# A hot expert's later tokens looked up straight from their ranks, with a new list of prologue steps

## The chip, the core and the metric

The program runs on one core of a Trainium2 chip. The metric is the time of one execution in microseconds (us) of device time, and lower is better. The kernel before has a median of 582.75 us over three runs (581.17 to 585.8).

The engines are TensorE (PE in the rows, and PEld for its weight loads), VectorE (DVE), ScalarE (ACT), GpSimd (POOL) and SyncE (SP). Each works through its own queue in order and waits for the others by semaphores. SyncE here mostly issues DMA transfers.

## The reference: an attention layer and two layers of experts

```python
kv = einsum('bhsd,bhse->bhde', k, v)            # 4 batches, 8 heads, 576 positions, 64 wide
out = einsum('bhsd,bhde->bhse', q, kv)
x = out / sqrt(mean(out * out, -1) + 1e-06) * g_norm   # then 2304 tokens of 512
# layer 1 (moe) and, on its result, layer 2 (moe2, with 576 places for each expert)
logits = x @ w_gate;  expert = argmax(logits);  gate = softmax(logits)[expert]   # 8 experts
out[tokens of e] = gate * (relu(x[tokens of e] @ w1[e]) @ w2[e])   # 512 -> 1024 -> 512
```

## The kernel before: attention as a listed prologue, then experts in blocks

Tokens lie in 18 units of 128 (UNITS, line 30): for each pair of batches eight units from the bodies and one from both tails. Units form four groups, 0-3, 4-8, 9-12 and 13-17 (GROUPS, line 28). A group shares one reciprocal root, one pass for the logits and one store of its rows to the tensor x1d in memory.

The prologue has no scheduler. ORDER (line 69) is a list of tokens; the loop at line 567 calls one small function for each, and the call appends its instructions to the queues of the engines. So the list sets the order on all engines at once. Names used below: Lk, Lv, Lq and Lt load k, v, q and the tails; kvB.P is one quarter of the product of k and v of batch B (10 matmuls, line 368); kvout, kvt, kvtc, kvg and kvgc prepare that product for use, with the gate's weights folded in (kvgc, line 392, is the last); oU is unit U's output (line 400), evU its evacuation (line 279 or 277), sqU the squares and ssqU their sums (lines 431 to 437); ra, rs, rb make the scale of a group (lines 449 to 463), lp and lg its logits (lines 478 and 485), st stores it. wN issues 2N matmuls whose result nobody reads. W loads a piece of expert weights, sh and sl split it into a high and a low part (lines 1105 and 1108).

Matmuls on expert weights are done as three products of such parts. Experts' tokens are done in blocks. Block 0 is 128 early tokens of the "hot" expert, the one most often chosen in the first nine units. `lead` (line 772, steps a) finds these tokens once groups 0 and 1 have logits: ranks come from a triangular matmul, and a one-hot lookup matmul (line 856) turns ranks into row numbers. Its weights' loads wait on SyncE's queue for the expert's number (ordia, line 839). The prologue also computes block 0: p (first product), t (turn), z (second product), y, lt, ll.

`final` (line 942, steps f) does all other tokens, once group 3 has logits (line 596 on): choice of expert, ranks for eight experts, each expert's rank and base, the one-hot tiles lo (line 647) and hv (line 658), the lookup matmuls (line 666), row numbers gi (line 677). Then block 1, the hot expert's next 224 tokens, is gathered from x1d (line 1137), normalised (nrm, line 1179), turned (xt, lines 1187 to 1199), and the loop of `moe` (line 1421) starts its matmuls at line 1211. That loop runs blocks 1, 2, ... of layer 1 and then layer 2, and steps generators such as `final` between the matmuls. Block 2 is the next expert's, of 320 tokens.

Of the kernel before, what the change touches and what calls it, by code (L numbers as in the profile page):

```python
# [70 lines left out]
Lk1.1 Lv1.1 Lv2.0 wgb kv1.0 kv1.2 ct2 Lq0.0 kvg0 eye Lk2.1 Lt2.0 iotawA kv1.3 kvout1A Lk2.0 foursD csD Lq1.0 triP
kvgc0 o2 ev2D Lq2.1 o1 Lq1.1 ev1A sq1A Lq2.0 o3 kvt1 kvtc1D ev3A o0 ssq1 kvg1 sq3A ssq3 ev0A sq0A kvgc1 o5 ev5A ssq0
sq2P o4 Lt0.1 ev4A ssq2 o6 ra0 rs0 rb0 ev6A sq6A ssq6 o7 sq5P Lt1.1 ev7A sq4A Lv2.1 ssq5 Lq3.1 kv2.1 kv2.0 o8 kv2.3
kv2.2 Lv3.1 lp0D sq7P ssq7 ev8A sq8A ssq4 ssq8 lg0 Lv3.0 st0 ra1 rs1 rb1 lp1D kvout2A w4.42386 kvt2 w1.42420 kvtc2A
w2.42371 kvg2 kvgc2 lg1 a1 o10 ev10A o9 st1 w1.42338 a2 w1.42406 ev9A a3 o11 o12 ev11A sq11P a4 a5 a6 ssq11 sq9A a7
Lk3.1 Lk3.0 kv3.1 kv3.0 kv3.3 kv3.2 sq10A ssq10 ssq9 Lq3.0 a8 ev12A sq12A W0 a9 firstD W1 ssq12 nrm0.0P Lt2.1 ra2 a10
w2.42387 kvout3D kvt3 kvtc3D rs2 rb2 w6.4256 lp2P kvg3 kvgc3 o13 W2 W3 f1 sh0 a11 sh1 ev13A o14 lg2 sl0 W4 sl1 W5
sq13P sh2 ev14A o16 ssq13 xt0.0 sl2 sh3 ev16D sq14P a12 ssq14 o17 ev17A sq16A ssq16 sl3 sq17A ssq17 sh4 w2.42422 o15
ev15A sq15A p0.0 sh5 a13 p0.1 st2 sl4 ssq15 ra3 rs3 p0.2 a14 rb3 sl5 W6 lp3P p0.3 lg3 f2 W7 t0.0 w4.42431 w3.42356 sh6
# [96 lines left out]
class Kernel:  # L176
# [109 lines left out]
    def attention(self):  # L286
# [3 lines left out]
        with ExitStack() as s:  # L290
# [157 lines left out]
            def ra(g):  # L448
                V.tensor_scalar(
                    out=small(0, g), in0=ssq[g].rearrange("p c h -> p (c h)"), scalar1=64e-6, scalar2=None, op0=ALU.add  # L450
                )

            def rs(g):
                A.activation(out=small(1, g), in_=small(0, g), func=ACTF.Sqrt)

            def rb(g):
                vv, r0, t = (small(i, g) for i in range(3))
# [1479 lines left out]
```

## Time and profile before

| what | us |
|---|---|
| median of three runs | 582.75 |
| the profiled execution | 584.3 |
| span in its profile, first to last instruction | 582.5 |
| TensorE busy in that span | 552.8 |
| first matmul on block 1 | 99.31 |

The profiled execution is 1.55 us above the median. The span splits at 99.31 us: ahead of it stands the prologue, whose order is written in the list; after it stands the loop over blocks.

### The profile page before, as it was taken

To read this page: it belongs to the slowest core of one execution; us is meant where nothing else is said; L and a number is where in the kernel's file an instruction comes from. 1 tells how busy PE (TensorE), PEld (TensorE's weight loads), DVE (VectorE), ACT (ScalarE), POOL (GpSimd) and SP (SyncE) were. 2 spreads that over 40 slices of the span, in tenths; PEclk is the share of its full clock that TensorE was granted. 3 is DMA by queue.
4 is the path that set the end of the run, shared out by engine and by line. 5 is a ranking of instruction groups with operands and counts; after the bars stand their busy time and mean duration, and the time that the engine had idled before them with its cause. 6 is when DMAs were issued, how large, how long until landed. Compare 5 with 4: busy or idle time off the path is not lost.

```text
span 582.5 us, 10758 instructions
## 1 busy us (share of the span) xinstructions
PE 552.8 (95%) x4130; PEld 525.1 (90%) x4130; DVE 330.2 (57%) x741; ACT 243.8 (42%) x421; POOL 182.4 (31%) x187
## 2 busy tenths in 40 slices
PE   8898898999999999999998999999999999999995
PEld 6887776998999999999987998989899999989994
DVE  0466983467867576767688586275147662211370
ACT  0456622436455555564645342244243532111440
POOL 1032225066625243433000101203322726543341
PEclk8999899999999999999999898999999999999998
DMA  9996746055556465656555434236234655768631
GB/s 305 399 381 217 264 144 193 3 178 168 179 172 205 157 203 172 213 176 200 175 181 166 134 111 167 72 93 234 88 101 153 202 188 177 257 238 265 242 127 39
DMA packets 34231, 106.89 MB, mean 184 GB/s; under 512 B 6665, under 2 KB 6795, under 8 KB 34172
## 3 DMA queue, kind: packets, MB, share of 16 engines
q1 hardware_dynamic: 24432, 81.90, 41.8%
q0 software_dynamic: 7072, 19.48, 10.7%
q10 hardware_dynamic: 2667, 4.75, 2.4%
q8 instruction: 34, 0.56, 0.4%
q14 instruction: 26, 0.20, 0.1%
HBM read 91.77 MB, written 14.60 MB: 183 GB/s over the span
## 4 chain that ended last, share of the span: by engine, by line
PE 69%; DVE 15%; issue 6%; ACT 5%; DMA 2%; POOL 1%; POOLq 0%; SPq 0%; ACTq 0%; DVEq 0%; another core or an unknown queue 0%
PE hps L1211 8%; PE hps L1212 8%; PE hps L1213 8%; PE acc L1211 7%; PE acc L1212 7%; PE acc L1213 7%; PE acc L1209 5%; PE hps L1209 4%; PE yps L1341 3%; DVE w1l L1108 3%; DVE w2l L1108 2%; PE xps L1187 2%; PE kv L368 2%; PE o L400 2%; PE sp L666 1%
## 5 line engine op out<-in xcount | busy, mean ns | idle before, releaser
L1211 PE MATMUL hps<-xh,w1h 128*128 128x256 f32 (+9 forms) x480 | 141.5, 295 | 1.0 <-ACT xh L1195 0.6
L1212 PE MATMUL hps<-xl,w1h 128*128 128x256 f32 (+9 forms) x480 | 139.0, 290 | 0.6 <-DVE xl L1199 0.5
L1213 PE MATMUL hps<-xh,w1l 128*128 128x256 f32 (+9 forms) x480 | 138.6, 289 | 0.0
L1232 ACT ACTIVATE hh<-hps 128x256 fp32r<-128x256 f32 (+12 forms) x144 | 54.4, 380 | 150.1 <-PE hps L1213 97.6
L1211 PE MATMUL acc<-hh,w2h 128*128 128x224 f32 (+8 forms) x352 | 104.6, 297 | 0.1
L1212 PE MATMUL acc<-hl,w2h 128*128 128x224 f32 (+8 forms) x352 | 103.0, 293 | 0.8 <-issue 0.8
L1213 PE MATMUL acc<-hh,w2l 128*128 128x224 f32 (+8 forms) x352 | 103.1, 293 | 0.0
L1211 PEld LDWEIGHTS hps<-xh,w1h 128*128 128x128 f32 x480 | 91.0, 190 | 3.0 <-issue 1.5
L1212 PEld LDWEIGHTS hps<-xl,w1h 128*128 128x128 f32 x480 | 91.1, 190 | 1.7 <-DVE xl L1199 1.3
L1213 PEld LDWEIGHTS hps<-xh,w1l 128*128 128x128 f32 x480 | 91.1, 190 | 0.0
L1234 DVE SCALAR_TENSOR_TENSOR hl<-hps,hh 128x256 fp32r<-128x256 f32 (+9 forms) x120 | 51.7, 436 | 63.7 <-ACT hh L1232 54.7
L1148 POOL DMA_INDIRECT xg<-x1d,gi x54 | 54.9, 1016 | 77.5 <-DVE xw L1162 63.5
L1108 DVE TENSOR_TENSOR w2l<-raw,w2h 128x1024 fp32r<-128x1024 f32 x52 | 66.2, 1276 | 19.2 <-ACT w2h L1105 18.1
L1396 POOL DMA_INDIRECT out_dram<-y,gi x44 | 50.5, 1149 | 70.9 <-DVE y L1392 56.8
L1108 DVE TENSOR_TENSOR w1l<-raw,w1h 128x1024 fp32r<-128x1024 f32 x52 | 64.0, 1248 | 13.6 <-ACT hh L1232 7.8
L1213 PEld LDWEIGHTS acc<-hh,w2l 128*128 128x128 f32 x352 | 67.2, 191 | 0.9 <-issue 0.9
L1211 PEld LDWEIGHTS acc<-hh,w2h 128*128 128x128 f32 x352 | 67.3, 191 | 0.3
L1212 PEld LDWEIGHTS acc<-hl,w2h 128*128 128x128 f32 x352 | 67.3, 191 | 0.2 <-issue 0.2
L1105 ACT ACTIVATE w2h<-raw 128x1024 fp32r<-128x1024 f32 x52 | 54.6, 1053 | 5.6 <-ACT y L1345 4.8
L1105 ACT ACTIVATE w1h<-raw 128x1024 fp32r<-128x1024 f32 x52 | 53.4, 1049 | 0.6 <-DMA raw<-in_moe_w_dram 0.5
L1137 POOL DMA_INDIRECT xg<-x2d,gi x21 | 20.0, 952 | 48.3 <-DVE gi L677 33.9
L1195 ACT ACTIVATE xh<-xps 128x512 fp32r<-128x512 f32 (+7 forms) x23 | 11.7, 512 | 45.3 <-PE xps L1187 31.2
(315 smaller groups left out, 818.9 us busy)
## 6 DMA issues: line engine op xcount, KB each, us to landing
raw<-in_moe_w_dram SPq DMA_DIRECT2D x104, 512.0 KB
w<-in_moe_w_dram SPq DMA_DIRECT2D x24, 512.0 KB
x1d<-xs POOLq DMA_DIRECT2D x4, 1056.0 KB
...
xg<-x1d,gi POOLq DMA_INDIRECT x59
```

What stands on the lines that cost most here:

```text
L1105: self.nc.scalar.activation(out=h, in_=t, func=ACTF.Copy)
L1108: self.nc.vector.tensor_tensor(out=l, in0=t, in1=h, op=ALU.subtract)
L1137: self.nc.gpsimd.indirect_dma_start(out=xg[:n], out_offset=None, in_=(self.X1, self.X2)[m][0:rows], in_offset=bass.IndirectOffsetOnAxis(ap ...
L1148: self.nc.gpsimd.indirect_dma_start(out=xg[:, g], out_offset=None, in_=(self.X1, self.X2)[m].rearrange("n (q x) -> (n q) x", q=4), in_offs ...
L1209: nc.tensor.matmul(out=out, lhsT=a[0], rhs=b[0], start=start, stop=stop)
L1211: nc.tensor.matmul(out=out, lhsT=a[0], rhs=b[0], start=start, stop=False)
L1212: nc.tensor.matmul(out=out, lhsT=a[0], rhs=b[1], start=False, stop=False)
L1213: nc.tensor.matmul(out=out, lhsT=a[1], rhs=b[0], start=False, stop=stop)
L1232: nc.scalar.activation(out=hh[:, fc, :], in_=ps, func=ACTF.Relu)
L1234: nc.vector.scalar_tensor_tensor(out=hl[:, fc, :], in0=ps, scalar=0.0, in1=hh[:, fc, :], op0=ALU.max, op1=ALU.subtract)
L1341: nc.tensor.matmul(out=ps[:n, j, :], lhsT=yt[:, dc, 128 * t:128 * t + n], rhs=self.iwg[:, dc, :], start=True, stop=True)
L1396: self.nc.gpsimd.indirect_dma_start(out=out, out_offset=bass.IndirectOffsetOnAxis(ap=rt["si4"][:, g - g0, t0 + t:t0 + t + 1].bitcast(U32), ...
```

## The change: what is looked up, when, and in which order

Four edits go together. First, `hot_block` finds the later tokens of the hot expert by itself: it needs only that expert's ranks, in two column groups (units 0-12, then 13-17), and its own lookup gives row numbers giq for block 1. The ranking of all experts follows after it in `final`, and its lookup and gi now come inside block 1; block 2 is then gathered from there. Second, the step ra is gone: the epsilon is a bias tile in the square root and an operand in rb. Third, the low part of a split may run on GpSimd, though every sl in the new list says D. Fourth, ORDER is another list; two of its lines stand in the diff. In it the constants iotaw (128x2944), first and eye are made on GpSimd, before on ScalarE, VectorE and GpSimd. The arrays' widths and the loop after block 2's first matmul are the same: each engine's queue holds the same instructions from there on.

```diff
--- before.py
+++ after.py
@@ -67,18 +67,19 @@ ORDER
-Lk0.1 Lv0.0 Lt1.0 Lv0.1 Lt0.0 Lk1.0 kv0.2 kv0.3 Lk0.0 w3.42407 kv0.1 kv0.0 kvout0D ct kvt0 kvtc0D Lv1.0 kv1.1 wg Lq0.1
...
+Lv0.1 Lk0.1 Lt0.0 Lt1.0 Lk0.0 Lv0.0 kv0.2 Lk1.0 kv0.3 Lv1.0 kv0.1 kv0.0 kvout0D ct kv1.1 kv1.0 Lk1.1 wg wgb Lv1.1
...
@@ -134,6 +135,9 @@
+HOT = (GROUPS[2][1], NCOL)
...
@@ -309,6 +314,7 @@
+            nc.gpsimd.memset(self.eps, 64e-6)
...
@@ -445,19 +451,18 @@
-            def ra(g):
-                V.tensor_scalar(
-                    out=small(0, g), in0=ssq[g].rearrange("p c h -> p (c h)"), scalar1=64e-6, scalar2=None, op0=ALU.add
+            def rs(g):
+                A.activation(
+                    out=small(1, g), in_=ssq[g].rearrange("p c h -> p (c h)"), func=ACTF.Sqrt, bias=self.eps
                 )
-            def rs(g):
-                A.activation(out=small(1, g), in_=small(0, g), func=ACTF.Sqrt)
...
-                V.tensor_tensor(out=t, in0=t, in1=vv, op=ALU.mult)
+                V.scalar_tensor_tensor(
+                    out=t, in0=ssq[g].rearrange("p c h -> p (c h)"), scalar=64e-6, in1=t, op0=ALU.add, op1=ALU.mult
+                )
...
@@ -510,8 +515,8 @@
-            def sl(_):
-                feed.low()
+            def sl(_, eng):
+                feed.low(eng)
...
@@ -939,6 +944,70 @@
+    def hot_block(self, hot, d, oh):
+        nc, V, t = self.nc, self.nc.vector, self.t
+        b = self.blocks[0][1]
+        nt = tiles_of(b.w)
+        val = self.tok1
+        own = t([128, NCOL], F16, "owna")
+        lo = self.mp.tile([128, 128, NCOL], F16, tag="yt", name="loq")
+        hv = self.rp.tile([128, 2, nt, NCOL], F16, tag="hvq", name="hvq")
+        for c0, c1 in zip((0,) + HOT, HOT):
+            n = c1 - c0
+            s = slice(c0, c1)
+            A3 = [128, n, E]
+            yield from self.chosen(0, c0, c1, d[:, s], oh[:, s])
+            w = t(A3, F32, "w")
+            V.tensor_tensor(out=w, in0=oh[:, s], in1=bc(hot, 1, A3), op=ALU.mult)
+            with nc.allow_low_precision("zeros and ones"):
+                V.tensor_reduce(out=own[:, s], in_=w, axis=AX.X, op=ALU.add)
+            yield
+            before = self.psum()[:, 0:c1 + n]
+            nc.tensor.matmul(out=before[:, c1:], lhsT=self.triw, rhs=own[:, s], start=True, stop=True)
+            nc.tensor.matmul(out=before[:, 0:c1], lhsT=self.onew, rhs=own[:, 0:c1], start=True, stop=True)
+            self.hold = True
+            yield
+            run = t([128, c1], F32, "runa")
+            V.tensor_tensor_scan(
+                out=run, data0=self.c(f"carry{c1}")[:, 0:c1], data1=before[:, 0:c1], initial=0.0,
+                op0=ALU.mult, op1=ALU.add,
+            )
+            rank = t([128, n], F32, "rank")
+            V.tensor_tensor(out=rank, in0=before[:, c1:], in1=run[:, s], op=ALU.add)
+            self.hold = False
+            yield
+            for i in range(nt):
+                V.scalar_tensor_tensor(
+                    out=hv[:, 0, i, s], in0=rank, scalar=128.0, in1=own[:, s], op0=(ALU.is_lt, ALU.is_ge)[i], op1=ALU.mult
+                )
+            low = t([128, n], F16, "low")
+            V.scalar_tensor_tensor(
+                out=low, in0=hv[:, 0, 1, s], scalar=-128.0, in1=rank, op0=ALU.mult, op1=ALU.add
+            )
+            yield
+            V.tensor_tensor(
+                out=lo[:, :, s], in0=self.iotaw[:, :, s], in1=bc(low, 1, [128, 128, n]), op=ALU.is_equal
+            )
+            yield
+            V.tensor_tensor(out=hv[:, 1, :, s], in0=hv[:, 0, :, s], in1=bc(val[:, s], 1, [128, nt, n]), op=ALU.mult)
+            yield
+        ps = self.psum()[:, 0:nt]
+        for j in range(NCOL):
+            nc.tensor.matmul(
+                out=ps, lhsT=lo[:, :, j], rhs=hv[:, 1, :, j], start=(j == 0), stop=(j == NCOL - 1)
+            )
+        self.hold = True
+        yield
+        gi = t([128, nt], I32, "giq")
+        V.tensor_scalar(out=gi, in0=ps, scalar1=float(OFF[0]), scalar2=None, op0=ALU.add)
+        self.hold = False
+        for i in range(nt):
+            n = min(128, b.w - 128 * i)
+            b.xgs.append((self.gather(0, gi, i, n), n))
+        yield
...
@@ -957,7 +1026,10 @@ final
-        yield from self.chosen(m, 0, ncol, d, oh)
+        if m == 0:
+            yield from self.hot_block(hot, d, oh)
+        else:
+            yield from self.chosen(m, 0, ncol, d, oh)
...
@@ -1019,7 +1091,9 @@
-        yield from self.index(m, rt, lo, hv, ncol, nt, "", self.blocks[m][-len(lay.blocks)].gather)
+        yield from self.index(
+            m, rt, lo, hv, ncol, nt, "", self.blocks[m][(2, -len(lay.blocks))[m]].gather
+        )
...
@@ -1444,7 +1518,7 @@ moe
-            if k and nb:
+            if k and nb and (m or "gi" in rt):
                 nb.gather()
...
@@ -1523,6 +1597,8 @@ moe
             if k == 1:
                 fin.run()
+                if not nb.xt:
+                    xs.extend(nb.x_steps())
...
```

What the new list does to the queues shows in three places. On TensorE, around the lookup of block 0 (ohe and triw are the ranks' operands, ot and lo the lookup's; kv_548 and kv_432 are the product of batch 3). Before, from the ranks of `lead` on:

```order
L794 MATMUL sp<-ohe,triw 128x72
L795 LDWEIGHTS onew
L795 MATMUL sp<-ohe,onew 128x72
L400 MATMUL o_117<-kvs,qkv 128x144 x4
L400 MATMUL o_116<-kvs,qkv 128x144 x4
L856 LDWEIGHTS lo_466
L856 MATMUL sp<-ot,lo_466 128x2
```

In the change, the same stretch:

```order
L374 MATMUL kv_432<-vtail,ktail 128x128
L393 MATMUL kt<-wgb,kts 128x16 x4
L799 LDWEIGHTS triw
L799 MATMUL sp<-ohe,triw 128x72
L800 LDWEIGHTS onew
L800 MATMUL sp<-ohe,onew 128x72
L374 MATMUL kv_432<-qkv 128x128 x4
L374 MATMUL kv_432<-vtail,ktail 128x128
L374 MATMUL kv_432<-qkv 128x128 x4
L374 MATMUL kv_432<-vtail,ktail 128x128
L406 MATMUL o_118<-kvs,qkv 128x144 x4
L861 LDWEIGHTS lo_426
```

Before, all of batch 3's product (line 368) stands behind the nine lookup matmuls; now two quarters stand ahead of the ranks and two between ranks and lookup.

On VectorE, from the last part of the lookup of block 1 to its row numbers (w2l is the low part of a weight split, hhl that of block 0's hidden values). Before:

```order
L1006 TENSOR_TENSOR tb<-oh_104,bcv 128x288
L647 TENSOR_TENSOR lo<-iotaw,low 128x2304
L1011 TENSOR_REDUCE btc<-tb 128x36
L1014 SCALAR_TENSOR_TENSOR tlf<-high,btc 128x18
L1016 TENSOR_TENSOR over<-rank,btc 128x18
L1018 SCALAR_TENSOR_TENSOR tl<-over,tlf 128x18
L658 TENSOR_TENSOR hv<-iotaw,tl 128x396
L659 TENSOR_TENSOR hv<-hv,ot 128x396
L1108 TENSOR_TENSOR w2l<-raw,w2h 128x1024
L1203 TENSOR_TENSOR hhl<-kt,hhl 128x4x128
L677 TENSOR_SCALAR gi<-sp 128x22
```

In the change:

```order
L965 TENSOR_REDUCE owna<-w 128x5
L1277 TENSOR_TENSOR hhl<-kt,hhl 128x4x128
L973 SCALAR_TENSOR_TENSOR runa<-ct,sp 128x18
L978 TENSOR_TENSOR rank<-sp,runa 128x5
L982 SCALAR_TENSOR_TENSOR hvq<-rank,owna 128x5 x2
L986 SCALAR_TENSOR_TENSOR low<-hvq,rank 128x5
L990 TENSOR_TENSOR loq<-iotaw,low 128x128x5
L994 TENSOR_TENSOR hvq<-hvq,ot 128x2x5
L1182 TENSOR_TENSOR w2l<-raw,w2h 128x1024
L1277 TENSOR_TENSOR hhl<-kt,hhl 128x4x128
L1004 TENSOR_SCALAR giq<-sp 128x2
```

The steps for all eight experts have left the way to the row numbers, and the tiles are of 5 columns instead of 18; the other 13 columns are done before group 3's logits.

On GpSimd, from group 3's logits to block 1's rows (misc is lp, x1d the store, xr the normalised rows). Before:

```order
L478 TENSOR_TENSOR misc<-xs_667 128x40x4 x2
L492 DMA x1d<-xs_667 512x1x528
L498 DMA x1d<-xs_667 64x528 x2
L1137 DMA xg<-x1d,gi 128x528
L1137 DMA xg<-x1d,gi 96x528
L1179 TENSOR_TENSOR xr<-xg 128x4x4x32
L1137 DMA xg<-x1d,gi 128x528 x2
```

In the change:

```order
L483 TENSOR_TENSOR misc<-xs_617 128x40x4 x2
L497 DMA x1d<-xs_617 512x1x528
L503 DMA x1d<-xs_617 64x528 x2
L1211 DMA xg<-x1d,giq 128x528
L1211 DMA xg<-x1d,giq 96x528
L1253 TENSOR_TENSOR xr<-xg 128x4x4x32
L1253 TENSOR_TENSOR xr<-xg 96x4x4x32
L1211 DMA xg<-x1d,gi 128x528 x2
```

Block 1's second 96 rows are now normalised here too (before on VectorE), and block 2's gathers, which need gi, stand behind them.

## Rows read from the trace of the kernel before

**Rows 1.** Stretches of 20 us: each engine's busy time, then clock, DMA share, GB/s

```profile
0.00:20.00 20.00, 16.03 (x105) 13.90 (x106) 3.67 (x11) 1.28 (x1) 2.42 (x11) 0.91 0.95 328
20.00:40.00 20.00, 19.18 (x164) 18.07 (x162) 11.78 (x29) 14.51 (x22) 4.31 (x5) 1.00 1.03 388
...
100.00:120.00 20.00, 20.00 (x185) 19.98 (x185) 8.99 (x29) 7.70 (x14) 3.60 (x5) 1.00 0.22 68
```

**Rows 2.** Chain of waits, prologue up to the last logits: start, us, what

```profile
8.55 3.79 PE kv L368 x20
...
17.24 3.35 PE kv L368 x30
...
22.61 3.15 PE o L400 x24
...
48.94 0.72 PE sp L856 x9
...
57.73 0.81 PE kt L387 x8
58.57 0.22 DVE kvs L392
...
76.53 0.50 DVE lg L485
```

**Rows 3.** Chain of waits, from the lookup to block 1's first matmul

```profile
86.83 1.74 PE sp L666 x18
88.59 0.19 DVE gi L677
...
89.05 6.18 DMA xg<-x1d,gi
95.37 1.05 POOL xr L1179
96.47 0.67 PE kv L1187 x4
97.16 0.70 ACT xh L1195
...
98.55 0.62 DVE xl L1199
...
99.31 0.34 PE hps L1211
```

**Rows 4.** VectorE in order of time: start, us, line, operation, idle time before

```profile
57.07 0.34 DVE L458 RECIPROCAL misc<-misc 128x32 f32<-128x32 f32 x1
...
60.03 3.20 DVE L1108 TENSOR_TENSOR w1l<-raw,w1h 128x1024 fp32r<-128x1024 f32 x2
...
65.54 0.81 DVE L279 COPY xs<-o 128x640 f32<-128x640 f32 x1
...
69.46 1.22 DVE L1108 TENSOR_TENSOR w2l<-raw,w2h 128x1024 fp32r<-128x1024 f32 x1
...
73.01 0.41 DVE L458 RECIPROCAL misc<-misc 128x40 f32<-128x40 f32 x1 [1.26 <-ACT misc L454]
...
77.05 0.30 DVE L596 TENSOR_REDUCE mx<-lg 128x18 f32<-128x144 f32 x1
...
83.67 1.42 DVE L647 TENSOR_TENSOR lo<-iotaw,low 128x2304 f16<-128x2304 f16 x1
```

**Rows 5.** GpSimd in order of time

```profile
12.17 0.61 POOL L279 COPY iwg<-ct 128x512 f32<-128x512 f32 x1 [9.89 <-DMA ct<-in_const_dram]
...
20.54 0.30 POOL L279 CAST triw<-ct 128x128 f16<-128x128 f32 x1 [7.71 <-DMA ct<-in_const_dram]
...
53.88 1.04 POOL L1179 TENSOR_TENSOR xr<-xg 128x512 f32<-128x512 f32 x1 [2.67 <-DMA xg<-x1d,gi0a]
...
74.55 1.95 POOL L478 TENSOR_TENSOR misc<-xs 128x160 f32<-128x160 f32 x2 [9.72 <-DVE xs L463]
```

**Rows 6.** SyncE's queue: the first load of expert weights

```profile
52.02 0.95 SPq L1131 DMA_DIRECT2D raw<-in_moe_w_dram  x2
```

More of the change, by code (lines that the diff above doesn't have):

```diff
@@ L69 @@
 ORDER = """
-Lk0.1 Lv0.0 Lt1.0 Lv0.1 Lt0.0 Lk1.0 kv0.2 kv0.3 Lk0.0 w3.42407 kv0.1 kv0.0 kvout0D ct kvt0 kvtc0D Lv1.0 kv1.1 wg Lq0.1
[L71 to L79, printed above, removed]
@@ new lines @@
+sq4P kv2.0 ssq4 triP sq5P ssq5 o8 ev8A sq8A ssq8 Lk2.1 o6 ev6D Lv2.1 o7 ev7A sq7A ssq7 kv2.1 Lk3.1 st0 Lk3.0 sq6A ssq6
+kv2.2 rs1 rb1 Lv3.1 Lq2.0 kv2.3 lp0P lg0 lp1D iotawP lg1 a1 kvout2A kv3.0 kvt2 firstP Lq2.1 kv3.2 kvtc2A kvg2 a2 kv3.1
+kvgc2 w4.13 kv3.3 o10 st1 a3 a4 a5 o11 kvout3A kvt3 w4.9 ev10A sq10P ev11A sq11P w3.10 a6 a7 a8 f1 o9 ev9A ssq10 o12
+kvtc3D sq9A ssq9 ev12A sq12A ssq11 ssq12 rs2 kvg3 Lq3.1 kvgc3 W0 rb2 w3.15 sh0 o16 sl0D a9 Lq3.0 o13 w2.6148 ev16A
+lp2P a10 lg2 f2 Lt2.1 o17 ev13A sq16A a11 W1 W2 sh1 f3 f4 sq13P ssq13 ssq16 f5 W3 f6 ev17A sh2 o15 W4 w4.18 o14 ev15A
@@ new lines @@
+sl1D sq17P ssq17 f7 f8 st2 sq15A sl2D ssq15 ev14A sh3 sl3D w2.6123 nrm0.0P w1.20 sq14A a12 w3.22 eye ssq14 xt0.0
+w4.6132 rs3 rb3 lp3P st3 f9 w1.19 lg3 f10 sh4 a13 w2.25 w4.6172 w3.6152 w1.6169 w6.6138 w4.6140 w1.6168 p0.0 w1.26
+p0.1 sl4D f11 a14 f12 f13 f14 p0.2 t0.0 p0.3 f15 z0.0 f16 f17 f18 f19 W5 sh5 sl5D t0.1 f20 z0.1 f21 z0.2 f22 nrm1.0P
+z0.3 W6 W7 sh6 sl6D sh7 nrm1.1P sl7D z0.4 z0.5 w6.6160 z0.6 z0.7 y0 w2.619 w1.6166 f23 w2.6163 lt0 f24 f25 f26 f27 f28
+f29 xt1.0 f30 w2.6131 ll0 xt1.1 f31 w1.32 f32 f33 w3.6128
@@ L156, in constants @@
     put("rev", 7 - e)
-    for n in sorted({NCOL, L1.cols, N // 128, *sum(EARLY, ())}):
+    for n in sorted({NCOL, L1.cols, N // 128, *sum(EARLY, ()), *HOT}):
         put(f"carry{n}", np.tile(np.arange(n) > 0, E))
@@ L204, in setup @@
         self.g = cp.tile([128, 1], F32, name="g")
+        self.eps = cp.tile([128, 1], F32, name="eps")
         self.wgt = cp.tile([128, DC, E], F32, name="wgt")
@@ L446, in small @@
                 return misc[:, o:o + count(g) * H]
[L448 to L454 removed]
+            def rs(g):
+                A.activation(
+                    out=small(1, g), in_=ssq[g].rearrange("p c h -> p (c h)"), func=ACTF.Sqrt, bias=self.eps
+                )
             def rb(g):
[L457 removed]
+                r0, t = small(1, g), small(2, g)
                 V.reciprocal(out=r0, in_=r0)
                 V.tensor_tensor(out=t, in0=r0, in1=r0, op=ALU.mult)
[L460 removed]
+                V.scalar_tensor_tensor(
+                    out=t, in0=ssq[g].rearrange("p c h -> p (c h)"), scalar=64e-6, in1=t, op0=ALU.add, op1=ALU.mult
+                )
                 V.tensor_scalar(out=t, in0=t, scalar1=-4.0, scalar2=12.0, op0=ALU.mult, op1=ALU.add)
@@ L562, in attention @@
                 f=lambda _: fin.step(), kv=kv, kvout=kvout, kvt=kvt, kvtc=kvtc, kvg=kvg, kvgc=kvgc, o=o, ev=ev, sq=sq,
-                ssq=sums, ra=ra, rs=rs, rb=rb, lp=lp, lg=lg, st=st, a=lambda _: lead.step(), W=lambda i: feed.load(i + 1),
+                ssq=sums, rs=rs, rb=rb, lp=lp, lg=lg, st=st, a=lambda _: lead.step(), W=lambda i: feed.load(i + 1),
                 Lt=load_tail, Lk=load_k, Lv=load_v, Lq=load_q, **self.consts(),
@@ L1105, in split_high, with split_low @@
         self.nc.scalar.activation(out=h, in_=t, func=ACTF.Copy)
-    def split_low(self, t, h, l):
-        self.nc.vector.tensor_tensor(out=l, in0=t, in1=h, op=ALU.subtract)
+    def split_low(self, t, h, l, eng="D"):
+        (self.nc.gpsimd if eng == "P" else self.nc.vector).tensor_tensor(out=l, in0=t, in1=h, op=ALU.subtract)
     def both(self, m, ev, kind, p):
@@ L1848, in high, with low @@
         self.nsplit += 1
-    def low(self):
+    def low(self, eng="D"):
         if self.half:
-            self.k.split_low(*self.half.pop(0))
+            self.k.split_low(*self.half.pop(0), eng)
 class Steps:
```

4 lines of the change are left out of this document (2 added, 2 removed).

## The prediction

> **What bounds the kernel now.** I read the stretches of 20 us first. From 100 to 120 us TensorE is busy 20.00 of 20 us; ahead of that it is not [rows 1]. From block 2's first matmul on, the change leaves every engine's queue as it was. So the time moves by as much as block 1's first matmul moves, now at 99.31 [rows 3], plus or minus what is done within block 1. The chain of waits was read next, backwards from that matmul: it waits for turned rows, these for a gather of 6.18 us, this for gi at 88.59, gi for 18 lookup matmuls of 1.74, and these for a VectorE chain that begins at group 3's logits, ready at 76.53 + 0.50 = 77.03 [rows 2, 3]. The logits come after a VectorE queue that begins with kvgc of batch 3 at 58.57, and this waits for kvg (57.73), which stands on TensorE behind the lookup of block 0 (48.94) [rows 2]. These are four legs, and I cost each.
>
> **Leg 1, to the end of kvgc 3: 58.79 now, 50.0 after.** What TensorE must do up to there is the same in both lists: 16 quarters of k·v, 13 units, four kvt, four kvg and lead's matmuls. A quarter takes 3.35 / 3 = 1.12, so 17.9; the first two took 3.79, which is 1.6 more; a unit takes 3.15 / 3 = 1.05, so 13.7; a kvg 0.81, so 3.2 [rows 2]. For kvt I take 0.5, an estimate below the 0.67 of four matmuls that turn rows [rows 3], so 2.0, and for lead 1.0: its lookup of 0.72 [rows 2] and two rank matmuls. The sum is 39.4. Before, it ran from 8.55 to 58.54 [rows 2], 50.0 us: 10.6 us were waits and filler matmuls. In the change the two quarters between ranks and lookup cover VectorE's part of lead, and two more stand ahead of the ranks, so that kvout, kvt and kvg of batch 3 wait for nothing of lead. I leave 1 us of waits and a start near 7.9, since k and v of the first quarter are now issued first: 7.9 + 39.4 + 1.0 = 48.3. The copy then stands behind VectorE's work on the last units (three passes over 512 columns, about 0.7 each by the 0.62 of xl [rows 3]), which adds 1.5; with its 0.22 it ends at 50.0. That is **8.8 earlier**. Could the loads be late instead? Up to v of batch 3 the list has 20 pieces of 0.52 MB and 2 MB of tails and constants, 12.5 MB. 20 us at 328 GB/s bring 6.6 MB, the rest at 388 GB/s takes 15.3 us [rows 1]: 35 us, about when these quarters come up. A loss of 0 to 2 us, taken as in the 1.
>
> **Leg 2, to group 3's logits: 18.24 now.** It is VectorE's queue. Added ahead of the logits: the 13-column half of the new lookup. Its 14 small operations cost 0.15 to 0.30 each (0.19 for gi, 0.30 for a reduction of 144 elements [rows 3, 4]); with the 13-column one-hot tile, 13/18 of 1.42 [rows 4], that is 3.1 to 5.2. I take 3.1, since small operations overlap their neighbours: 14 times 0.15 and 1.0. Also added: group 2's scale, which now stands behind the copy and not ahead of it, 58.57 - 57.07 = 1.5 [rows 2, 4], taken 1.4, and two operations of the gate, 0.4. Gone: one w2l of 1.22, the evacuation of unit 16 (0.81, to ScalarE), the making of "first", about 0.7, the addition of epsilon, 0.2, and the wait of 1.26 for the square root [rows 4], since more work stands ahead of it now. 3.1 + 1.4 + 0.4 - 1.2 - 0.8 - 0.7 - 0.2 - 1.3 = **0.7 longer**; bounds -0.6 and 3. Logits at 50.0 + 18.9 = 68.9; I say 69.0.
>
> **Leg 3, to the row numbers: 88.78 - 77.03 = 11.75 now.** The change's queue on VectorE from the logits to giq, as the order shows it: hvq 0.2, w2l 1.2, two operations of Ga 0.3, eight on 40 elements, each between 0.15 and 0.30, at 0.2: 1.6, hhl 0.65 (as xl [rows 3]; it covers the rank matmuls), scan and rank 0.4, three for hvq and low 0.5, the one-hot tile 5/18 of 1.42 = 0.4, hvq 0.2; then 18 lookup matmuls, 1.74, beside which w2l and hhl take 1.9; giq 0.2. The sum is 7.55. **4.2 shorter**; bounds 3 and 5.
>
> **Leg 4, to block 1's first matmul: 99.31 - 88.78 = 10.5 now.** The gathers read the same bytes in the same two pieces. Both normalisations are on GpSimd now, 1.05 each [rows 3], one after the other, where the second ran beside the first. The second turning writes the bank of the first and waits for its evacuation, about a matmul group and a pass of 0.67 + 0.70 [rows 3] of which half lay bare before. I add **1.5**; bounds 0.3 and 2.5.
>
> Together: -8.8 + 0.7 - 4.2 + 1.5 = -10.8; rounded against me for the many small waits, 10.5: block 1's first matmul at 88.8. **Leg 5** is given back in block 1: all experts' ranking now runs there, and its 18 lookup matmuls stand in a full TensorE stream, 1.6 to 1.74 [rows 3]; what VectorE does for it moves other small work toward block 2's start, which I put at 0.5, between 0 and 2. So the gain is 10.5 - 1.6 - 0.5 = 8.4. The profiled execution took 584.3, 1.55 above the median of 582.75; 584.3 - 8.4 = 575.9, in terms of the median **574.3**.
>
> **At nothing:** the fillers, fewer now, lie in waits. The eps memset is at the start, the operand in rb is in an operation that ran anyway. iotaw on GpSimd has 2944 columns: between 2.6 us (the slope from 0.30 for 128 columns to 0.61 for 512) and 6.9 (2.3 ns a column, from the 128 alone) [rows 5]. I take 3.0, nearest to the larger row. Its first reader, the one-hot tile of lead, comes near 41.8, with 1 to 5 us to spare. At 6.9 lead slips up to 2 us; of that kvg 3 feels nothing, the weights do. SyncE: the last quarter's q and the q tail stand behind the first weight load, which waits for lead's expert number. It was issued at 52.02 [rows 6]; I expect 45, and units 13 and 17 are needed near 50.
>
> **A lock between two engines.** VectorE's two w1l at 60.03 took 3.20, and w2l at 69.46 alone 1.22: beside GpSimd's squares the pair lost 0.76 [rows 4]. The Trainium skill, "SBUF — State Buffer", section "Who interferes with whom", says that a VectorE operation with two inputs in SBUF and a GpSimd operation that reads SBUF exclude each other for a whole instruction, so that the loser stands still. It speaks against this change, which gives GpSimd iotaw and a normalisation. By the row I charge nothing more, since the squares were there before. If every such meeting cost its full length, the added GpSimd work in these legs would be one normalisation of 1.05, a tile of 0.61 (iwg's size), and at most 2.0 of iotaw [rows 3, 5]: 3.7 less gain, 578.0.
>
> **Rivals.**
> (a) That exclusion, in full: 578.0, within 1%. For it is the 0.76; against it, that most of this work lies ahead of the copy, where TensorE sets the time. 0.12.
> (b) The loads of q 3 and its tail come late because lead isn't earlier: first weight load at 52 as before, units 13 and 17 at 54 or later. Then 4 of leg 1's 8.8 are lost: 578.5. For it, their place in the queue; against, that lead's own logits come from units which the list does not delay. 0.08.
> (c) The clock. Its granted share was 0.91 in the first 20 us, where TensorE was busy 16.03, and 1.00 from 20 to 40, at 19.18 [rows 1]. If it drops to the lower of its levels in the thinner stretch near 60 to 88, block 0's matmuls take up to twice as long; most hide behind VectorE. 576.5. 0.05.
> (d) The gather is faster: that of block 0 landed 2.67 after its issue ended [rows 5], where block 1's took 6.18 with two issues [rows 3]. With 3 less, 571. 0.08.
> (e) **Slower.** Block 2's rows. Their numbers were ready at 88.59, 10.7 before block 1 began; now they come inside it. Block 1 is 192 matmuls of 20.00 / 185 = 0.108 [rows 1], 20.8 us, so from 88.8 it ends near 111 with the lookup. The rows must be in by 107 to be turned. I expect the lookup near 93 and three gathers behind it, landing between 97 and 103. Each us beyond 107 stands bare on TensorE. Slower by over 1% takes 8.4 + 5.8 = 14.2, so rows landing past 121: VectorE, full of splits in block 1, would have to put off the ranking by 18 us. At 122 the time is 589. For it, the ranking's long list of small steps, which are taken one per slot; against, the 4 to 10 us to spare. 0.07.
>
> **The numbers.** The forecast's own mechanism, all five legs as costed, has 0.60. Its leg bounds give 570 to 578: leg 2 alone can take 2.3, leg 4 give 1.2, leg 5 take 1.5. With (d) below and (a) to (c) above, 568.5 to 580.0 leaves (e) and a part of the ends out. A measurement of this kernel tells about 1%, 5.8 us, from no change. Under 576.9 lie most of the forecast, (d) and (c): 0.72. Within 1% the rest of the forecast, (a) and (b): 0.21. Slower: 0.07.
>
> **What would show it.** In the profile of the changed kernel kvgc 3 should stand near 50, group 3's logits near 69, giq near 76.5, block 1's first matmul near 88.8, and 18 lookup matmuls of 1.6 to 1.74 inside block 1, with under 1 us of idle TensorE before block 2. kvgc at 54 with a late q load means (b); w1l of 1.6 and more each, or iotaw over 6 us, (a); matmuls of batch 3 at twice their length, (c); idle TensorE after 108, (e). I'm wrong altogether if block 1's first matmul comes early but TensorE's busy time behind it grows by more than the lookup.

## The result: 5.3 us faster, and the profile after

The changed kernel has a median of 578.12 us over 20 runs, the kernel before, timed beside it, 583.38 over 20. The ratio is 0.9909, with a 95% interval of 0.9884 to 0.9933: between 3.9 and 6.8 us are gained. Forecast were 8.4 and 574.3, with a range from 568.5 to 580.0 that holds the measured time. The chances leaned to a larger gain: 0.72 stood on more than 1% and 0.21 on less, and the measured 0.91% has an interval that reaches to both sides of 1%. The profiled execution took 577.17, its span is 575.0.

The legs, each from the named end to the next (the first column from [rows 2, 3], the last from the rows below):

| leg | before | forecast | after |
|---|---|---|---|
| 1, to the end of kvgc 3 | 58.79 | 50.0 | 51.55 |
| 2, to group 3's logits | 18.24 | 18.9 | 21.15 |
| 3, to the row numbers of block 1 | 11.75 | 7.55 | 7.1 |
| 4, to block 1's first matmul | 10.5 | 12.0 | 10.0 |
| block 1's first matmul | 99.31 | 88.8 | 89.79 |
| 5, given back up to block 2 | | 2.1 | 3.7 |

VectorE of the changed kernel in order of time (start, us, line, operation, idle time before), which answers to [rows 2, 4]:

```profile
51.33 0.22 DVE L398 COPY kvs<-kt 128x64 f32<-128x64 f32 x1
...
55.83 0.95 DVE L602 TENSOR_TENSOR d<-lg,mx 128x104 f32<-128x104 f32 x1
...
59.20 0.79 DVE L963 TENSOR_TENSOR w<-oh,hot 128x104 f32<-128x104 f16 x1
60.02 0.26 DVE L965 TENSOR_REDUCE owna<-w 128x13 f16<-128x104 f32 x1
...
72.21 0.49 DVE L490 TENSOR_REDUCE lg<-misc 128x40 f32<-128x320 f32 x1 [0.94 <-POOL misc L483]
...
79.66 0.15 DVE L1004 TENSOR_SCALAR giq<-sp 128x2 int32<-128x2 f32 x1
...
112.05 0.15 DVE L1128 TENSOR_TENSOR o<-run,bcv 128x8 f32<-128x8 f32 x1
...
116.27 0.17 DVE L1175 CAST tokw<-aux 128x23 f16<-128x23 f32 x1
116.36 1.21 DVE L1182 TENSOR_TENSOR w1l<-raw,w1h 128x1024 fp32r<-128x1024 f32 x1
117.50 0.74 DVE L1273 SCALAR_TENSOR_TENSOR xl<-xps,g,xh 128x512 fp32r<-128x512 f32 x1
119.65 0.48 DVE L1273 SCALAR_TENSOR_TENSOR xl<-xps,g,xh 128x256 fp32r<-128x256 f32 x1 [1.41 <-ACT xh L1269]
```

The copy ends at 51.55, the logits at 72.70, giq at 79.81. Two operations of the 13-column half took 0.95 and 0.79 where owna, a reduction over the same 104 elements with one input, took 0.26. Twenty small operations run from 112.05 to 116.44, and the split w1l and the low parts xl of block 2's rows stand behind them.

TensorE of the changed kernel:

```profile
30.44 0.46 PE L374 MATMUL kv<-vtail,ktail 128*128 128x128 f32 x2 [2.00 <-DMA ktail<-in_k_tail_dram]
...
54.94 1.20 PE L411 MATMUL o<-kvs,qtail 128*64 128x144 f32 x16 [0.65 <-ACT xs L282]
60.35 0.20 PE L968 MATMUL sp<-owna,triw 128*128 128x13 f16 x1 [4.21 <-DVE owna L965]
...
60.42 3.75 PE L406 MATMUL o<-kvs,qkv 128*128 128x144 f32 x16
...
92.54 1.72 PE L671 MATMUL sp<-hv,lo 128*128 128x44 f16 x18
...
119.67 0.41 PE L1285 MATMUL hps<-xh,w1h 128*128 128x320 f32 x1 [2.69 <-ACT xh L1269]
...
151.43 0.31 PE L1285 MATMUL hps<-xh,w1h 128*128 128x312 f32 x1
```

In leg 1 the longest wait was 2.00 us, for the load of a tail of k (30.44). There is a wait that I had not seen: 4.21 us for the own columns (owna), with units 15 and 14 queued behind. The lookup of all experts stands in block 1 (92.54). Ahead of block 2 TensorE waits 2.69. The last row is block 3's first matmul. The same places of the kernel before:

```profile
125.51 0.41 PE L1211 MATMUL hps<-xh,w1h 128*128 128x320 f32 x1 [0.61 <-ACT xh L1195]
...
157.64 0.30 PE L1211 MATMUL hps<-xh,w1h 128*128 128x312 f32 x1
```

Block 1's first matmul is 9.5 us earlier, block 2's 5.8 and block 3's 6.2. From there the queues are the same, and the medians' gain, 5.3 between 3.9 and 6.8, agrees with that.

Stretches of the changed kernel (columns as in [rows 1]):

```profile
56.00:60.00 4.00, 0.14 (x4) 0.00 (x0) 3.85 (x10) 2.48 (x3) 1.83 (x3) 1.00 0.60 241
60.00:64.00 4.00, 3.65 (x18) 3.65 (x19) 3.87 (x9) 1.24 (x2) 2.19 (x3) 0.57 0.75 251
...
89.79:128.06 38.27, 34.86 (x295) 33.58 (x296) 19.25 (x61) 12.55 (x24) 19.22 (x20) 1.00 0.42 136
354.00:357.00 3.00, 3.00 (x11) 2.52 (x10) 1.40 (x6) 0.60 (x1) 0.00 (x0) 0.50 0.00 0
```

TensorE idled from 56 to 60 and was granted 0.57 of its clock in the next 4 us, mostly the lower level, 1.2 GHz: 3.75 us for two units that took 2.21 at the full one (e7). The third row ends at the 40th matmul of block 2: 3.41 us idle. The kernel before, with a stretch of its prologue ahead and then over the same matmuls:

```profile
66.00:70.00 4.00, 3.59 (x20) 3.56 (x20) 3.97 (x8) 3.28 (x5) 0.00 (x0) 0.68 0.98 337
...
99.31:132.62 33.31, 32.59 (x278) 31.98 (x278) 17.54 (x54) 12.25 (x23) 14.07 (x14) 1.00 0.31 97
...
320.00:323.00 3.00, 3.00 (x17) 3.00 (x16) 1.81 (x9) 0.11 (x1) 1.93 (x2) 0.51 0.58 190
361.00:364.00 3.00, 3.00 (x16) 2.71 (x14) 1.34 (x6) 0.60 (x1) 0.00 (x0) 0.50 0.04 14
```

It has a thin clock too, 0.68 from 66 to 70, so that the change's 0.57 is no cost of the change alone. Over the same matmuls it takes 4.96 us less, for the same work without the lookup, with 0.72 idle. The two profiles also differ, in the part with equal queues, by one stretch of 3 us at half the clock (two before, one after). By the rows that is about 1.5 us of the spans' difference, an estimate, and no effect of the change.

GpSimd of the changed kernel:

```profile
34.33 2.74 POOL L284 CAST iotaw<-ct 128x2944 f16<-128x2944 f32 x1
...
55.62 1.04 POOL L437 TENSOR_TENSOR sq<-xs 128x512 f32<-128x512 f32 x1 [0.57 <-ACT xs L282]
58.83 1.04 POOL L437 TENSOR_TENSOR sq<-xs 128x512 f32<-128x512 f32 x1 [2.17 <-DVE misc L443]
...
84.43 2.17 POOL L1253 TENSOR_TENSOR xr<-xg 128x512 f32<-128x512 f32 x2 [1.33 <-DMA xg<-x1d,giq]
```

iotaw took 2.74 (3.0 forecast). The two squares begin at 55.62 and 58.83, and the two long VectorE operations beside them end 0.12 us after them. And the chain of waits ahead of block 1:

```profile
83.88 0.25 PE kv L1287
...
84.15 0.70 ACT y L1365
84.89 0.66 PE kv L1374 x4
85.55 0.66 PE kt L1261 x4
...
86.95 0.75 DVE xl L1273
87.70 1.33 DVE lo L652
89.11 0.55 DVE xl L1273
...
89.79 0.34 PE hps L1285
```

It runs through block 0's last product and its output, no longer through the gather (landed at 84.43). The rows were normalised soon after 85.5, just when TensorE turned to them at 85.55, so the two paths end together and neither alone sets the start. The one-hot tile lo of all experts stands bare between the two xl.

### The profile page after: what moved, and what is told of

The parts are those of the page before. It is cut to its first block, busy times and chain, and to the rows that moved or that the text cites. A ratio compares the mean times of both kernels' runs of the same rounds, so it can differ in the third digit from the quotient of the medians.

```text
span 575.0 us, 10693 instructions
## 1 busy us (share of the span) xinstructions
PE 542.9 (94%) x4082; PEld 517.0 (90%) x4082; DVE 332.5 (58%) x755; ACT 241.7 (42%) x421; POOL 189.8 (33%) x195
## 4 chain that ended last, share of the span: by engine, by line
PE 67%; DVE 12%; issue 6%; DMA 6%; ACT 6%; POOL 1%; another core or an unknown queue 1%; SPq 1%; POOLq 0%; ACTq 0%; DVEq 0%
PE hps L1286 9%; PE hps L1285 9%; PE hps L1287 9%; PE acc L1285 7%; PE acc L1287 7%; PE acc L1286 7%; PE acc L1283 5%; PE hps L1283 5%; PE yps L1415 3%; DMA qkv<-in_v_dram 3%; DVE w1l L1182 2%; PE xps L1261 2%; DMA vtail<-in_v_tail_dram 2%; DVE w2l L1182 2%; PE sp L671 1%
## 5 line engine op out<-in xcount | busy, mean ns | idle before, releaser
L1182 DVE TENSOR_TENSOR w2l<-raw,w2h 128x1024 fp32r<-128x1024 f32 x52 | 63.4, 1221 | 19.9 <-ACT w2h L1179 17.7
L1283 PE MATMUL acc<-hh,w 128*128 128x176 f32 (+2 forms) x192 | 28.7, 301 | 2.4 <-issue 2.4
```

The costliest lines, as they stand in the source:

```text
L1182: (self.nc.gpsimd if eng == "P" else self.nc.vector).tensor_tensor(out=l, in0=t, in1=h, op=ALU.subtract)
L1283: nc.tensor.matmul(out=out, lhsT=a[0], rhs=b[0], start=start, stop=stop)
```

## The experiments

All ratios are to the kernel before, run on the same chip beside the experiment. "Block 1" and "block 2" are their first matmuls in the profile. The kernel before has a median of 583.3 beside e1 to e4, 581.7 beside e5 to e8 and 580.5 beside e9 to e12, so medians of different rows are not to be subtracted; the ratios are. Places in single profiles differ by as much as 1.6 us without a cause in the edit: e4 has the change's queues up to block 1 and starts it at 91.40 against 89.79.

| kernel | median, us | ratio, 95% interval | block 1 | block 2 |
|---|---|---|---|---|
| the change | 578.12 | 0.9909, 0.9884 to 0.9933 | 89.79 | 119.67 |
| e1, list alone | 585.78 | 1.0054, 1.0023 to 1.0086 | 98.23 | 124.44 |
| e2, ranks behind units | 577.64 | 0.9897, 0.9863 to 0.9930 | 89.83 | 119.04 |
| e3, batch 3 late again | 585.37 | 1.0051, 1.0018 to 1.0084 | 98.31 | 126.76 |
| e4, small steps early | 574.29 | 0.9855, 0.9809 to 0.9901 | 91.40 | 118.43 |
| e5, list alone, mended | 578.15 | 0.9927, 0.9895 to 0.9960 | 96.33 | 122.39 |
| e6, e2 and e4 | 572.40 | 0.9834, 0.9784 to 0.9885 | 90.35 | 117.38 |
| e7, fillers in the wait | 575.67 | 0.9899, 0.9849 to 0.9949 | 91.88 | 120.26 |
| e8, two squares moved | 574.93 | 0.9882, 0.9819 to 0.9945 | 91.12 | 118.15 |
| e9, batch 3 alone early | 586.08 | 1.0109, 1.0061 to 1.0158 | 106.02 | 131.48 |
| e10, epsilon alone | 580.15 | 1.0011, 0.9981 to 1.0041 | 99.89 | 125.99 |
| e11, e4's edit, before | 581.38 | 1.0041, 1.0007 to 1.0075 | 99.15 | 124.79 |
| e12, e6 and e8 | 569.67 | 0.9840, 0.9795 to 0.9885 | 88.54 | 115.57 |

**Leg 1: e3 and e9.** In the change's list:

```diff
- ... a1 kvout2A kv3.0 kvt2 ... kv3.2 kvtc2A kvg2 a2 kv3.1 kvgc2 w4.13 kv3.3 o10 st1 a3 a4 a5 o11
+ ... a1 kvout2A kvt2 ... kvtc2A kvg2 a2 kvgc2 w4.13 o10 st1 a3 a4 a5 kv3.0 kv3.2 kv3.1 kv3.3 o11
```

> As the change, but all four quarters of batch 3's product stand behind the lookup of block 0 again, as before. Theory A, that their place is the main term: TensorE idles 3 to 4 us in lead's chain and has 4.5 us of quarters behind the lookup, the last copy of batch 3 ends near 55 and not 51.5, block 1's first matmul near 93, the time 3 to 4 us above the change's. Theory B, that the copy's earliness is lost again later in VectorE's queue: the copy is late by 3 to 4 but block 1 by less than 1.5, and the time is within 1 us of the change's.

The copy ended at 60.18, the logits came at 81.20, and the whole gain was gone. Theory A holds, and the loss was twice what it gave: the copy is 8.6 later and block 1 8.5. TensorE in e3 shows why:

```profile
46.03 0.70 PE L861 MATMUL sp<-ot,lo 128*128 128x2 f16 x9 [1.83 <-DVE lo L828]
46.59 2.06 PE L374 MATMUL kv<-qkv 128*128 128x128 f32 x8
...
48.87 1.91 PE L374 MATMUL kv<-qkv 128*128 128x128 f32 x8
```

After waiting in lead's chain it ran the first quarters at half the clock (0.53 granted from 45 to 52), 2.06 for 1.06. So a part of the loss is the clock's, and e3 doesn't part it from that of the place. The converse, batch 3's tokens alone moved in the old list:

```diff
- ... Lv3.0 ... lg1 a1 o10 ... a2 w1 ev9A ... a7 Lk3.1 Lk3.0 kv3.1 kv3.0 kv3.3 kv3.2 sq10A ... ssq12 ... kvout3D kvt3 kvtc3D ... kvg3 kvgc3
+ ... Lv3.0 Lk3.1 Lk3.0 ... lg1 kv3.1 kv3.0 a1 o10 ... a2 kv3.3 kv3.2 ev9A ... a7 kvout3D kvt3 kvtc3D sq10A ... ssq12 kvg3 kvgc3
```

> The kernel before, with its own list, in which batch 3's product alone is moved: loads and two quarters ahead of lead's ranks, two quarters behind the ranks, and what follows of it sooner. Nothing else of the change. Theory A, that this place on TensorE is the main term by itself: the last copy of batch 3 ends near 51 to 53 and not 58.8, the last logits 4 to 7 us sooner, block 1's first matmul near 93 to 95, the time 4 to 6 us under the kernel before. Theory B, that the rest of the old list holds the gain back (weights for block 0, which wait for lead's number as before): the copy is sooner, block 1 by less than 3 us.

Neither: it was 1.1% slower. VectorE in e9:

```profile
48.08 0.30 DVE L802 TENSOR_TENSOR_SCAN run<-ct,sp 128x72 f32<-128x72 f32 x1 [3.57 <-PE sp L795]
```

With two quarters and two units ahead of the rank matmuls lead waited 3.57 us for TensorE, the first weight load went out at 55.34 (52.02 in [rows 6]), and the clock was 0.50 to 0.56 from 54 to 65. Nor did the copy come sooner: it ended at 59.22 (58.80 before), though the quarters were done at 50.3 and not at 54.2. On VectorE kvout of batch 3 stood behind lead's last step, and TensorE waited for it:

```profile
55.11 1.12 PE L378 MATMUL kt<-ct,kvs 128*128 128x128 f32 x4 [2.39 <-DVE kvs L279]
```

So the early place gives nothing without the rest of the new list. Lead's own logits are earlier there, at 40.38 in the change and 43.36 before, but no run shows that alone to be the reason.

**Leg 2: e2 and e7.** In e2 the rank matmuls of the first 13 columns stand behind the units:

```diff
- f5 W3 f6 ev17A sh2 o15 W4 w4.18 o14 ev15A
+ f5 W3 ev17A sh2 o15 W4 w4.18 o14 f6 ev15A
```

> As the change, but the two rank matmuls of the first 13 columns stand behind units 15 and 14 on TensorE. Theory A, that TensorE's wait of 4.21 us for these columns makes the last logits late: units 15 and 14 start near 56.3 and not 60.4, the last logits come near 69.5 to 70.5 and not 72.7, block 1's first matmul near 87, the time 2 to 3 us under the change's. Theory B, that VectorE's own queue sets the last logits: they stay within 0.7 us of 72.7 and the time is the same.

TensorE in e2:

```profile
55.31 1.25 PE L406 MATMUL o<-kvs,qkv 128*128 128x144 f32 x8
...
57.27 1.15 PE L406 MATMUL o<-kvs,qkv 128*128 128x144 f32 x8
59.59 0.18 PE L968 MATMUL sp<-owna,triw 128*128 128x13 f16 x1 [1.18 <-DVE owna L965]
```

The units came some 5 us sooner, the logits 1.1 (71.63), block 1 not at all (89.83). The last two differ from the change by less than equal queues do (1.6), and the ratio is the change's within its interval, so the logits' queue feels little of TensorE's wait: the outcome is nearer to theory B. The chain of e2 names what comes next:

```profile
60.69 4.69 DMA raw<-in_moe_w_dram
65.38 0.66 ACT xhl L1269
...
66.05 1.28 ACT L455
```

A piece of block 0's weights lands at 65.4, and on ScalarE's queue what waits for it stands ahead of the last group's square root (1.28 of table load). Block 1's rows landed a microsecond sooner than in the change (83.38 for 84.43), but block 0's second product ran at a clock of 0.50 from 78 to 80 and held block 1. In e7 the wait is left and filled:

```diff
- f5 W3 f6 ev17A
+ f5 W3 w18 f6 ev17A
```

> As the change, with 36 more filler matmuls on TensorE ahead of the rank matmuls of the first 13 columns, where it waited 4.21 us, and then did units 15 and 14 in 3.62 us at a granted clock of 0.5 (2.2 at 1.0). Theory A, that the idle stretch is what the clock fell after: units 15 and 14 take 2.2, the last logits come 1.4 sooner, at 71.2; block 1, held by block 0's products, moves by 0 to 1.4. Theory B, that the clock falls there in any case, or falls a little later instead: the two units may take 2.2, but a stretch at 0.5 stands elsewhere ahead of block 1, and block 2 starts within 0.7 of 119.67. The time is within 1 us of the change's by either.

Two stretches of e7:

```profile
57.00:61.00 4.00, 4.00 (x42) 3.43 (x39) 3.83 (x11) 2.76 (x4) 1.83 (x2) 1.00 0.65 258
61.00:65.00 4.00, 3.71 (x31) 2.99 (x29) 3.86 (x10) 2.02 (x4) 2.46 (x4) 1.00 0.67 235
80.00:83.00 3.00, 3.00 (x10) 2.02 (x9) 3.00 (x6) 0.83 (x1) 1.77 (x1) 0.51 0.00 0
```

The clock stayed full at the units (2.21 for both), and a low stretch stood at 80, in block 0's second product. That is theory B, and the ratio is the change's within its interval. But e2, with the wait cut down and not filled, has its low stretch there too, so it is not shown that the filling moved it.

**Legs 3 and 5: e1, e5, e4, e11.** e1 has the new list with the lookup and the root of the kernel before, whose f2 to f18 stand in the places of f11 to f21:

```diff
- lg2 f2 ... f10 ... f11 a14 f12 f13 f14 p0.2 t0.0 p0.3 f15 z0.0 f16 f17 f18 f19 W5 ... f20 z0.1 f21 z0.2 f22 ... f33
+ lg2 ... f2 a14 f3 f4 f5 p0.2 t0.0 p0.3 f6 z0.0 f7 ... f16 W5 ... f17 z0.1 f18 z0.2
```

e5 moves its scan ahead of t0.0:

```diff
- f2 a14 f3 f4 f5 p0.2 t0.0 p0.3 f6 z0.0 f7 ... f16 W5
+ f2 a14 f3 f4 f5 p0.2 f6 f7 f8 f9 f10 t0.0 p0.3 f11 f12 f13 z0.0 f14 f15 f16 W5
```

> The new list of steps, with the lookup of all experts left as before (no steps for the hot expert alone, epsilon added by itself). Theory A, that the early copy of batch 3's product carries the gain and the hot expert's own lookup pays for itself only just: the last logits come 3 to 5 us sooner than in the change (68 to 70, the 13-column half and TensorE's wait for it are gone), row numbers 11.7 later near 80.5 to 81.5, block 1's first matmul near 91, no lookup inside block 1 and 0.6 us of idle TensorE ahead of block 2: block 2 begins near 117.5, 2 us ahead of the change (119.67), and the time is 1 to 3 us under the change's. Theory B, that the lookup is the gain: block 1 starts at 94 or later, block 2 after 121, and the time is 2 us or more above the change's.

> The new list with all experts looked up before block 1, as the run before of this kind, but VectorE's scan and ranks stand ahead of the low part of block 0's hidden values, which held them up for 3.27 us there. Theory A, that the hot expert's own lookup is worth what it takes out of VectorE's queue ahead of block 1, less what comes back inside block 1: row numbers come near 81.5 and not 84.9, block 1's first matmul near 95, block 2 near 121, between 0.5 and 3 us behind the change (119.67); the time is 579 to 582. Theory B, that the gain of the own lookup seen there (7.7 us) was real in full: block 1 stays at 98 and the time at 585.

The logits came at 69.41 and 69.51, 3.2 sooner than in the change, as expected. In e1 VectorE then waited for a hidden value of block 0:

```profile
75.73 0.69 DVE L1204 TENSOR_TENSOR hhl<-kt,hhl 128x512 fp32r<-128x512 f32 x1 [3.27 <-ACT hhl L1196]
```

By e1's own words that is its theory B: block 1 at 98.23, block 2 at 124.44, and a ratio 1.5% above the change's. But a part of it was my placement: e5, where this wait is 1.01, is 1.3% faster than e1 by their ratios, and theory B of e5 falls. The own lookup starts block 1 6.5 us sooner (96.33 against 89.79) and gives most of it back inside block 1: block 2 is 2.7 sooner. The list alone (e5, 0.9927) and the whole change (0.9909) can't be told apart by their times; the own lookup is ahead only with the small steps early (e6 below, 0.9784 to 0.9885 against e5's 0.9895 to 0.9960). The list alone with the small steps early was not run. The edit of e4 takes these steps earlier within block 1:

```diff
-A1, A2, B1, ... = 1.078, 2.417, 1.15, ...
+A1, A2, B1, ... = 1.078, 3.6, 1.15, ...
```

> As the change, but within block 1 more small steps are taken per slot (3.6 for 2.4 in its second half), so that the last small VectorE operations stand ahead of the splits and of the low parts of block 2's rows. Theory A, that these operations make TensorE wait ahead of block 2: idle time there falls from 2.69 us to 0.6 to 1.3, the time by 1.4 to 2.1. Theory B, that the wait comes from elsewhere (the third transposition's signal arrived 2.1 us after its matmuls ended): it stays at 2 us or more, and the time is the same.

One stretch of e4, over the same matmuls as above:

```profile
91.40:125.09 33.69, 33.69 (x295) 33.46 (x296) 20.73 (x62) 13.11 (x24) 15.14 (x15) 1.00 0.47 151
```

No idle time is left: 33.69 where the change took 38.27. This holds in every pair: without the edit the change, e2, e3, e7 and e8 took 37.2 to 38.3 over these matmuls, with it e4, e6 and e12 took 33.7, and the three pairs of ratios (the change and e4, e2 and e6, e8 and e12) differ by 0.4 to 0.6%. The 4.6 that it takes away are 3.41 of idle time and 1.17 in which the same 295 matmuls stand as busy for longer. The other 0.4 of the change's 4.96 over the kernel before is the lookup, 1.1 us of busy time (33.69 less 32.59), less the 0.7 of waits that the kernel before had. Theory A, and more than it gave.

How VectorE's tail holds TensorE is seen best in e8 (below), whose queues within block 1 are the change's, and where block 2's rows were turned in time:

```profile
119.01 1.13 DVE L1273 SCALAR_TENSOR_TENSOR xl<-xps,g,xh 128x512 fp32r<-128x512 f32 x2
...
120.20 0.41 PE L1286 MATMUL hps<-xl,w1h 128*128 128x320 f32 x1 [1.73 <-DVE xl L1273]
```

The last small operation ended at 117.95, a split of 1.21 stood behind it, and only then came xl, for which TensorE waited 1.73. The same edit on the kernel before:

> The kernel before with more small steps per slot inside block 1, as in the run with early small steps. Theory A, that the wait ahead of block 2 was brought by the change: here it was 0.61 us, so at most 0.6 to 0.8 is to be had there, and with the wait of 1.43 within block 2 at most 2; the time is 0 to 2 us under the kernel before. Theory B, that early small steps help either kernel alike: 3 to 4 us under the kernel before.

It gained nothing, and is if anything a little slower (1.0007 to 1.0075). Neither theory has a loss; A, that the waits are the change's own, is the nearer.

**The lock: e8.** Two squares go to ScalarE.

```diff
-... f3 f4 sq13P ssq13 ... o14 ev15A sl1D sq17P ssq17
+... f3 f4 sq13A ssq13 ... o14 ev15A sl1D sq17A ssq17
```

> As the change, but the squares of units 13 and 17 are on ScalarE and not on GpSimd. In the change VectorE's d took 0.95 us and w 0.79, each beside one of these squares on GpSimd, where like operations took 0.27. Theory A, that the two engines exclude each other: d and w take 0.25 to 0.3 here, 1.2 us less, and the other operations beside a GpSimd product stay long. Theory B, that they were long for another reason: they stay over 0.6. The time: ScalarE has 1.3 us more to do in the same stretch, so within 1.5 us of the change's either way.

VectorE in e8:

```profile
55.86 0.27 DVE L602 TENSOR_TENSOR d<-lg,mx 128x104 f32<-128x104 f32 x1
...
58.70 0.26 DVE L963 TENSOR_TENSOR w<-oh,hot 128x104 f32<-128x104 f16 x1
```

0.95 and 0.79 became 0.27 and 0.26 with the squares gone, while two hvq beside GpSimd's normalisation of block 0 stayed at 0.97 together (0.91 in the change), and low beside its copy of iwg at 0.47. Theory A. The Trainium skill, "SBUF — State Buffer", section "Who interferes with whom", says that a VectorE operation with two inputs in SBUF contends with a GpSimd operation that reads SBUF, and that the contention is an exclusive lock. The trace agrees: in the change each of the two ended 0.12 us after the square beside it. The logits came no sooner (73.6): ScalarE had the squares, and VectorE waited 2.15 us for one of them.

**Epsilon alone: e10**, on the kernel before.

```diff
-V.tensor_scalar(out=small(0, g), in0=ssq[g]..., scalar1=64e-6, ...)
-A.activation(out=small(1, g), in_=small(0, g), func=ACTF.Sqrt)
+A.activation(out=small(1, g), in_=ssq[g]..., func=ACTF.Sqrt, bias=self.eps)
```

> The kernel before with the epsilon folded into the square root and the step that added it taken out; nothing else. Theory A, as costed: 0.2 us less in VectorE's queue ahead of each group's root, so block 1 begins 0 to 0.4 us sooner and the time is within 0.2% of the kernel before. Theory B, that the 1.26 us wait for ScalarE's root hung on that step: the wait falls under 0.8 and block 1 begins 0.5 to 1.2 us sooner.

No difference in time, so theory A; block 1 was 0.6 later in this profile, within what such profiles differ by. The wait for the root was 0.36 here and nothing in e11, which has the step still: the 1.26 of [rows 4] came with that one execution.

**Together: e6 and e12.**

> As the change, with both mended: the rank matmuls of the first 13 columns behind units 15 and 14, and the last small VectorE operations of block 1 ahead of the splits. Theory A, that the two waits are independent: block 2 begins near 117 to 118 with no idle TensorE ahead of it, and the time is 573 to 575, that is the 3.8 of the second and the 0.5 of the first. Theory B, that block 0's second product on TensorE sets block 1's start either way: the time equals that of the kernel with early small steps alone, 574.3, within 0.7.

> As the change, with three mends: rank matmuls of the 13 columns behind units 15 and 14, early small steps in block 1, and the squares of units 13 and 17 on ScalarE. Theory A, that each takes away a wait of its own: block 2 begins near 116.5 and the time is 0.5 to 1.5 us under that of the first two mends (0.9834 of the kernel before). Theory B, that ScalarE, with 1.3 us more, then holds the last logits: the time is the same as with two mends, within 0.3%.

e6, the list with e2's and e4's edits, stands at 0.9834: faster than the kernel before, and 0.8% under the change's 0.9909, their intervals touching only at the ends. Block 2 began at 117.38 with no idle time ahead of it. Whether e2's edit starts block 1 sooner is open: 90.35 lies between the change's 89.79 and e4's 91.40, and e6's ratio is within e4's interval. e12 is the same by its ratio (theory B), though its profile has block 2 at 115.57; whether the third mend adds anything is open.

## Why the prediction was right, and where it was off

- **What bounds it** held: the time moved with block 1's start and what was given back up to the 40th matmul of block 2, 9.5 less 5.0, that is 4.6 beside the medians' 5.3.
- **Leg 1** (7.2 of 8.8 gained) was the right term, and e3 shows that undoing it alone costs everything. The sum of matmuls held: TensorE was busy for 38.8 of the 39.4 forecast. It began at 6.3 and not 7.9, and its waits were 4.4 and not 1. Of these, 4.0 were for loads, which the prediction put at "0 to 2".
- **Leg 2** was mis-sized: 2.9 longer, forecast 0.7, its bound 3. Without the 13-column half the leg took 17.25 (e1, e5), so the half cost 3.9 and not 3.1, and the rest of the leg 1.4 more than the sum had for it. Of the first, the small operations were priced at 0.15 each as if alone, and two of them met GpSimd for 1.2 (e8). Of the second, the wait of 1.26 for the root, counted as gained, was none of the list's: it is 0.36 in e10 and none in e11, whose legs are 17.1 and 17.0 with the queues of before. I also did not follow the rank matmuls of the own columns into TensorE's queue, where two units stood behind them. But with either cause taken away (e2 20.8, e8 22.0) the leg is no shorter than profiles differ by (e4 22.2, with the change's queues), so what else sets it is open.
- **Leg 3** held (7.1 for 7.55).
- **Leg 4** was 2.0 shorter than forecast. The gather was faster: rows there 4.6 after the row numbers and not 6.5, 1.9 of rival (d)'s 3. With that, block 0's output, which I had not counted on this path, ends together with the rows, and in e2, where the rows came sooner, block 1 did not.
- **Leg 5 is the step that failed.** The lookup cost no more than costed (1.1 of busy time in e4). The step that "moves other small work toward block 2's start, which I put at 0.5, between 0 and 2" was 2.1 at block 2's first matmul and 4.6 up to its 40th, by e4, which removes all of it. Its sign, "under 1 us of idle TensorE before block 2", failed with 2.69. Behind that, block 2 runs 1.65 shorter to block 3 than in the profile of before (23.37 for 25.02), but that is not the change's doing: e10, with the queues of before, took 23.36. The errors ahead of it cancelled by luck: legs 1 and 2 together were 3.8 too long, legs 3 and 4 2.5 too short and the rounding took 0.3, so that block 1 came at 89.79 for 88.8.
- **Rivals.** (a) was half right: the lock is real, about 1.2 us at two operations, but not what decides (e8); that its 578.0 is the measured time is chance. (b): the load went out at 47.05 (45 forecast); no unit waited for it. (c): the clock did fall, for units 15 and 14, which took 1.5 longer; but the kernel before has such a stretch from 66 to 70, so this is no loss against it, and in e7, without it there, the time is the same. (e): block 1 takes 25.6 us and not the 20.8 that were reckoned (99.31 to 125.51 before, less the wait of 0.61), so there was more room than I thought. The numbers came at 94.48, the rows in time; not they, the small steps behind them made TensorE wait.

Left open: in the change ScalarE's third xh began at 119.14, although its turning matmuls stand at 114.99. That is 3.7 us after their end; it was 0.2 in e4, and 0.4 in e8, whose queues there are the change's. So part of the 2.69 is not the small steps', and no run tells what held it.
